# Loads of the next tokens' x2 issued singly and earlier in the projection, and one x tile split ahead of W's evictions

## The chip, the core and the metric

The kernel runs on one core of one Trainium2 chip. The metric is device time of one execution in microseconds (us), the median of several runs. All figures here come from those runs and from one profiled execution of the kernel. Engines are named as the profile names them: PE (TensorE matmuls), PEld (its weight loads), DVE (VectorE), ACT (ScalarE), POOL (GpSimd) and SP (SyncE, which here only issues DMAs).

## The reference

Three stages follow one another on 3072 tokens (4 batches of 768) with a model width of 512:

```
scores = q k^T / sqrt(64) + bias, kept only for the 8 global keys and the 96 local ones
x   = softmax(scores) v                       # 8 heads of 64, put side by side: 3072 x 512
x2  = (((x w1) * (x w2)) w3) w_out            # 512 -> 1024 -> 1024 -> 512
h   = x2 w_in                                 # 512 -> 2048
out = (h * cos(h)) w_out2                     # 2048 -> 512
```

Everything is float32.

## The kernel before, in words

**Precision.** Each float32 operand is split into a high and a low part in the format fp32r, and a product is three matmuls (high by high, high by low, low by high), issued by `mm3` (L419 in the rows). A split is a cast on ACT for the high part and a subtraction, nearly always on DVE, for the low part.

**First stage.** The weights w3 and w_out are multiplied into one matrix W (loop over `c` in `chunks`, 16 steps; `wmm` at L869 is its matmul, L877 and L878 are the ACT cast and the DVE subtraction that evict W). Attention for the first units (a unit is 128 tokens of two heads) runs in the same loop. `a_out` (L658 the ACT cast, L659 the DVE subtraction) splits a finished x tile of 384 tokens into the operand `xT`. In the loop's last step (`c` = 15) the program order on ACT and DVE is: the normalisation of one unit (`a_norm`; L599 and L602 on DVE, then L608 on ACT), W's four evictions, one decoding step of a weight (`decode`; L343 and L344 on ACT), and then `a_out` of the fourth x tile of the first token block. The next stage starts with `up`, whose twelve matmuls (four k by three) read the four x tiles in turn.

**Second stage.** Eight blocks of 384 tokens go through x w1, x w2 and W, while the remaining attention units and the decoding of w_in and w_out2 run beside them. x2 is written to DRAM (`x2s`).

**Third stage.** The tokens are taken in three passes `q` of 1024 tokens. Both products use a seven-product (Strassen) form on 2 x 2 blocks. In each pass:

- `phase_a` (eight steps k) computes h and the gate h * cos(h). Its right operands are B11, B22, B21 (blocks of x2) and T1 to T4 (their combinations), each in split form. They stand in single buffers.
- `phase_b`, the projection, walks the list `turn` of 56 pairs (n, k), called turns here. A turn is six matmuls. Turns 14 to 20 write to `k_ps`, turns 21 and 22 to `h_ps`, turn 23 to `k_ps`, and turn 24 begins a new product in `h_ps`. The left operand is a piece of w_out2 of 512 KB, which serves two turns; the right operand is `op`, made by `op_split` four turns ahead in program order (L1222 the ACT cast, L1223 the DVE subtraction), in a ring of six buffers. `fold` (L1240) forms the sums that later turns need.

In `phase_b` at turn `at`, the program order is: `pieces_to` (L1140 on SP: sends the piece of six pairs of turns ahead, once a buffer of its ring of eight is free), `op_split` of turn `at` + 4, the folds and gates due at this turn, the x2 work described next, and then the turn's matmuls, with an eviction where a product ends (`evict`).

**The x2 work.** The operands of the next pass are prepared inside `phase_b` of the passes 0 and 1. At turn 14 `x2_loads` sends B11, B22 and B21 (L933, 512 KB each) and then B12 into the buffer `r0` (L1365, 512 KB), all on SP. `x2_steps` is a list of 18 steps, each one instruction on DVE or ACT: first r1 = B22 - r0 (L959, it needs B22 and B12), then r0 = r0 - B11, and then the splits of B11, T1, T2, T3, B21, B22 and T4 (L946 on ACT, L948 on DVE). One step is taken at each of the turns 16, 21, 28 and every turn from 37 on but 44, 45 and 48. `r0` and `r1` take the two buffers that the last two gates of `phase_a` used; the gates' DVE multiplications that read them stand at turns 8 and 12.

All engines work through their instructions in the written order, so an instruction that waits holds up all that follow it on its engine. SP is in that respect an engine too.

Of the kernel before, what the change touches and what calls it, by code (L numbers as in the profile page):

```python
# [32 lines left out]
K1, M1, MO = DM // 128, DF1 // 128, DM // 128  # L33
# [238 lines left out]
def fused(ctx, tc, a_qk, a_v, a_v0, w3p, wo1p, w1p, w2p, winp, wo2p, out):  # L272
# [477 lines left out]
    with tc.manual_schedule():  # L750
# [8 lines left out]
        for o in "3A3A3A3A3A3A3A3ABBBBBBBB":  # L759
# [3 lines left out]
            else:  # L763
                n, m = ups.pop(0)
# [67 lines left out]
        def decode(n):  # L832
            for _ in range(n):
                next(steps_left, None)
# [27 lines left out]
        for c, (h, k) in enumerate(chunks):  # L862
            n = c - 1
            own = n if n < LEAD else -9
            if k == 0:
                W_ps = {m: p_mm.tile([128, 512], F32, tag="mm", name="mm") for m in range(4)}

            def wmm(m):
                nc.tensor.matmul(  # L869
                    W_ps[m], lhsT=wt["w3", c][:, m * 128:(m + 1) * 128], rhs=wt["wo1", k],  # L870
                    start=k == 0, stop=k == M1 - 1,
                )
                if k == M1 - 1:
                    t = wt["W", 4 * h + m] = wts.tile(
                        [128, 2, 512], F32R, tag="Wb" if h else "Wa", name="W", bufs=4
                    )
                    nc.scalar.copy(out=t[:, 0, :], in_=W_ps[m])  # L877
                    nc.vector.tensor_tensor(  # L878
                        out=t[:, 1, :], in0=W_ps[m], in1=t[:, 0, :].bitcast(F32), op=ALU.subtract
                    )  # L880

            a_load(own + 3)
            a_load_v(n - 1 if n > 2 else -1)
            if c % 3 == 0 and c < 12:
                bias_heads(*dists, range(2 * c // 3, 2 * c // 3 + 2))
            elif c == 10:
                tp.release()
            if n > 0:
                a_scores(own)
            if n > 0:  # L890
                a_load_plain(own + 2)
            a_values(n - 3)
            a_max(own)
            if c == 2 * M1 - 1:
                a_norm(n - 1, True)
                for m in range(4):
                    wmm(m)
            decode(1)
            a_out(n - 3)
            a_split_hi(own + 2)  # L900
            a_exp(own)
            a_split_lo(own + 2)
            if c < 2 * M1 - 1:
                wmm(0)
                wmm(1)
            a_transpose(n - 2)
            a_tcopy(n - 2)
            decode(1)
            if 1 <= n < 2 * M1 - 2:
                a_norm(n - 1, True, lambda: decode(1))  # L910
            else:
                decode(2)
            decode(2 if c < 8 else {14: 1, 15: 2}.get(c, 3))
            if c < 2 * M1 - 1:
                wmm(2)
                wmm(3)
# [8 lines left out]
            c = slice((2 * q + half) * TB2, (2 * q + half + 1) * TB2)  # L925
            return x2s[rows:rows + 2, :, c].rearrange("k p t -> p k t")

        def x2_loads(q):
            for name in ("B11", "B22", "B21"):
                t = x2c[name] = x2_pool[name].tile(  # L930
                    [128, 2, 2, TB2], F32R, tag=name, name=name, bufs=1
                )
                nc.sync.dma_start(out=t[:, :, 1, :].bitcast(F32), in_=x2_cols(name, q))  # L933
# [55 lines left out]
        for j in range(NB1):  # L989
            for i in range(UPB):  # L990
                sl = j * UPB + i
                n = sl + LEAD
# [71 lines left out]
        def one_bank():  # L1064
            return p_h.tile([128, TB2], F32, tag="h", name="h_ps")
# [207 lines left out]
        def phase_b(q):  # L1273

            final = q == NQ - 1
            base = (2 * q + 1) * (NP * 7 // 2)
            ps = {}
            extra = last_gates()
            for k in range(NP):
                for at, what in folds(k).items():  # L1280
                    extra[at] = extra.get(at, []) + what
            x2_next = None
            kept = {}

            def raw():
                return misc.tile([128, 2, TB2], F32, tag="raw", name="res", bufs=3)

            def total(out, p, q):
                nc.vector.tensor_tensor(out=out, in0=p, in1=q, op=ALU.add)

            def place(half, e):
                rows = slice(half * 256, half * 256 + 256)
                t = out[rows, (2 * q + e) * TB2:(2 * q + e + 1) * TB2]
                return t.rearrange("(i p) c -> p i c", p=128)

            def keep(name, t):

                kept[name] = t
                for i in range(2):
                    nc.scalar.copy(out=t[:, i, :], in_=ps["a"][i])  # L1300

            def evict(n):

                if n == 0:
                    keep("p0", raw())
                elif n == 1:
                    keep("p01", late.tile([128, 2, TB2], F32, tag="sum", name="sum", bufs=1))
                elif n == 4:
                    o = kept["p0"]
                    total(o, ps["c"], o)  # L1310
                    nc.sync.dma_start(out=place(0, 0), in_=o)
                elif n == 2:
                    keep("p012", raw())
                    o = raw()
                    for i in range(2):
                        total(o[:, i, :], ps["d"][i], kept["p012"][:, i, :])
                    nc.sync.dma_start(out=place(1, 1), in_=o)
                elif n == 5:
                    o = kept["p012"]
                    total(o, ps["b"], o)  # L1320
                    nc.sync.dma_start(out=place(0, 1), in_=o)
                elif n == 6 and not final:
                    o = kept["p01"]
                    for i in range(2):
                        total(o[:, i, :], ps["d"][i], o[:, i, :])
                    nc.sync.dma_start(out=place(1, 0), in_=o)

            def evict_last(i):

                o = kept["p01"]  # L1330
                for h, queue_ in enumerate((nc.scalar, nc.sync)):
                    c = slice(h * 256, h * 256 + 256)
                    total(o[:, i, c], ps["d"][i][:, c], o[:, i, c])
                    queue_.dma_start(out=place(1, 0)[:, i, c], in_=o[:, i, c])

            def step(n, k, which):
                bank = home_of[n]
                w = pieces[q, n, k // 2][:, k % 2]
                x = ops[n, k]
                for i in which:  # L1340
                    if k == 0 and n in opens and i == 0:
                        if bank in "ad":
                            ps[bank] = [one_bank(), one_bank()]
                        else:
                            t = two_banks()
                            ps[bank] = t
                    mm3(
                        ps[bank][i] if bank in "ad" else ps[bank][:, i, :],
                        [(w[:, i, 0, :], w[:, i, 1, :], x[:, 0, :], x[:, 1, :])],
                        n in opens and k == 0, k == NP - 1, n not in opens,  # L1350
                    )

            for at, (n, k) in enumerate(turn):
                pieces_to(base + pairs_of.index((n, k // 2)) + 6)
                if at + 4 < len(turn):
                    op_split(*turn[at + 4])
                for what in extra.get(at, ()):
                    what()
                if at == 14 and not final:
                    x2_loads(q + 1)  # L1360
                    r0, r1 = (
                        late.tile([128, 2, TB2], F32, tag="x2f", name="x2f", bufs=2)
                        for _ in range(2)
                    )
                    nc.sync.dma_start(out=r0, in_=x2_cols("B12", q + 1))  # L1365
                    x2_next = x2_steps(r0, r1)
                if x2_next and (at in (16, 21, 28) or at > 36 and at not in (44, 45, 48)):
                    some(x2_next, 1)
                if q == 0 and at in (34, 38, 42):
                    flags_of[0] = next(steps_f)  # L1370
                if final and at >= len(turn) - 4:
                    if at == len(turn) - 1:
                        for i in range(2):
                            for kk in range(NP - 4, NP):
                                step(n, kk, (i,))
                            evict_last(i)
                else:
                    step(n, k, range(2))
                    if k == NP - 1:
                        evict(n)  # L1380
            return x2_next
# [95 lines left out]
```

## Time and profile before

| What | us |
|---|---|
| median of 3 runs (lowest to highest) | 1095.5 (1094.88 to 1096.44) |
| the profiled execution, its own time | 1096.8 |
| its span, first to last instruction | 1094.9 |
| PE busy | 1073.8 (98%) |
| DVE busy | 832.1 (76%) |
| ACT busy | 731.4 (67%) |
| POOL busy | 237.5 (22%) |
| mean granted TensorE clock | 0.993 |

The span is cut by stages: the first ends at about 93 us, the second at about 615 us, and the third fills the rest. Within the third, `phase_b` of pass 0 runs from about 691 to 776 us and that of pass 1 from about 852 to 936 us. A granted clock of 1.00 is 2.4 GHz, one of 0.50 is 1.2 GHz.

### The profile page before, as it was taken

The page shows a single profiled execution, that of the slowest core. Times are in us where ns is not written, and L with a number is a line of the kernel's source. Part 1 is how long each engine was busy: PE and PEld are TensorE (multiplying, and loading weights), DVE is VectorE, ACT ScalarE, POOL GpSimd, SP SyncE. Part 2 cuts the span into 40 slices and gives each one's busy share as a digit, 9 for nine tenths or more (in the row PEclk, how much of TensorE's full clock was granted, in tenths as well). Part 3 has the DMA queues.
Part 4 walks back from the last instruction along what each step waited for, and adds up shares of the span by engine and source line. Part 5 has one row for each costly group of instructions (what it writes and reads, how often), then busy time and mean ns, then how long its engine had stood idle before and what let it go on. Part 6 is the DMA issues. An engine that isn't in the chain of part 4 may idle for free.

```text
span 1094.9 us, 17774 instructions
## 1 busy us (share of the span) xinstructions
PE 1073.8 (98%) x5922; PEld 933.1 (85%) x5922; DVE 832.1 (76%) x1812; ACT 731.4 (67%) x1487; POOL 237.5 (22%) x249
## 2 busy tenths in 40 slices
PE   8999999999999999999999999989999989999997
PEld 5557899999999999999999988868888868888886
DVE  8887767878788787787826388868788869688984
ACT  7998867777677676676734388736378736478652
POOL 0000011111211111121100078300078200178100
PEclk9999999999999999999999999989999989999999
DMA  9865466666666756666452456564855565855563
GB/s 332 287 192 171 142 200 200 204 227 197 221 202 204 239 189 221 200 213 212 138 193 95 144 192 192 188 219 168 292 194 194 175 240 190 276 192 193 173 195 115
DMA packets 88308, 219.24 MB, mean 200 GB/s; under 512 B 9488, under 2 KB 26384, under 8 KB 88208
## 3 DMA queue, kind: packets, MB, share of 16 engines
q1 hardware_dynamic: 87696, 217.44, 59.5%
q8 instruction: 49, 0.80, 0.3%
q10 hardware_dynamic: 512, 0.58, 0.2%
q14 instruction: 51, 0.42, 0.1%
HBM read 176.04 MB, written 41.94 MB: 199 GB/s over the span
## 4 chain that ended last, share of the span: by engine, by line
PE 55%; DMA 2%; DVE 1%; ACT 1%; issue 0%; POOL 0%; DVEq 0%; ACTq 0%; POOLq 0%
PE h_ps L419 36%; PE mm L419 11%; PE k_ps L419 5%; DMA x2f<-x2s 1%; PE x_ps L644 1%; PE pt_ps L617 0%; DMA o2s<-ap 0%; PE pt_ps L619 0%; PE s_ps L559 0%; PE s_ps L555 0%; DVE x2f L959 0%; ACT e L589 0%; DVE op L1223 0%; ACT raw L344 0%; DVE xT L659 0%
## 5 line engine op out<-in xcount | busy, mean ns | idle before, releaser
L419 PE MATMUL h_ps<-op,piece 128*128 128x512 f32 x720 | 171.4, 397 | 9.8 <-DVE op L1223 9.8
L610 POOL TENSOR_SCALAR e<-e,st 128x232 f32<-128x232 f32 x148 | 76.1, 525 | 476.9 <-DVE st L602 385.0
L419 PEld LDWEIGHTS h_ps<-op,piece 128*128 128x128 f32 x720 | 137.8, 192 | 39.7 <-DVE op L1223 10.6
L419 PE MATMUL mm<-xT,wA 128*128 128x384 f32 x768 | 146.8, 340 | 0.5 <-ACT xT L658 0.4
L419 PE MATMUL mm<-xT,wB 128*128 128x384 f32 x768 | 146.2, 339 | 0.0
L419 PE MATMUL mm<-ab,W 128*128 128x384 f32 x768 | 146.2, 340 | 0.0
L419 PE MATMUL h_ps<-T,piece 128*128 128x512 f32 x576 | 138.4, 389 | 0.0
L419 PEld LDWEIGHTS mm<-xT,wA 128*128 128x128 f32 x768 | 130.9, 188 | 3.2 <-issue 1.8
L419 PEld LDWEIGHTS mm<-ab,W 128*128 128x128 f32 x768 | 131.1, 188 | 2.4 <-issue 2.4
L419 PEld LDWEIGHTS mm<-xT,wB 128*128 128x128 f32 x768 | 130.9, 188 | 2.1 <-issue 2.1
L419 PEld LDWEIGHTS h_ps<-T,piece 128*128 128x128 f32 x576 | 108.1, 188 | 22.5
L1113 POOL TENSOR_TENSOR gr<-r,gr 128x1024 f32<-128x1024 f32 x21 | 50.5, 2405 | 290.5 <-ACT r L1108 289.0
L419 PE MATMUL h_ps<-B,piece 128*128 128x512 f32 x432 | 105.7, 389 | 0.0
L419 PEld LDWEIGHTS h_ps<-B,piece 128*128 128x128 f32 x432 | 81.1, 188 | 16.8
L589 ACT ACTIVATE e<-e,top 128x232 f32<-128x232 f32 (+1 forms) x192 | 89.3, 467 | 2.2 <-DVE top L578 2.1
L522 ACT CAST hh<-qk 128x720 fp32r<-128x720 f32 x74 | 58.9, 796 | 46.7 <-PE s_ps L559 42.5
L578 DVE CUSTOM_DVE_ANT_0 e<-s_ps,bias 128x232 f32<-128x232 f32 (+1 forms) x192 | 64.9, 374 | 14.3 <-PE s_ps L559 8.6
L419 PE MATMUL k_ps<-op,piece 128*128 128x512 f32 x288 | 67.9, 392 | 0.0
L419 PEld LDWEIGHTS k_ps<-op,piece 128*128 128x128 f32 x288 | 54.9, 191 | 11.6
L869 PE MATMUL mm<-wo,w 128*128 128x512 f32 x128 | 61.2, 606 | 1.1 <-DVE wo L360 1.1
L1105 ACT ACTIVATE r<-r 128x1024 f32<-128x1024 f32 x48 | 51.0, 1062 | 16.6 <-DVE r L1099 16.6
L1222 ACT CAST op<-gr 128x512 fp32r<-128x512 f32 x72 | 42.9, 621 | 28.3 <-PE h_ps L419 11.2
(136 smaller groups left out, 1968.6 us busy)
## 6 DMA issues: line engine op xcount, KB each, us to landing
piece<-a_s SPq DMA_DIRECT2D x84, 512.0 KB, 4.2
piece<-o2s SPq DMA_DIRECT2D x84, 512.0 KB, 3.9
qk<-in_a_qk SPq DMA_DIRECT2D x74, 360.0 KB, 3.4
a_s<-ap SPq DMA_DIRECT2D x56, 256.0 KB, 2.5
o2s<-ap SPq DMA_DIRECT2D x56, 256.0 KB, 2.5
v<-in_a_v SPq DMA_DIRECT2D x95, 128.0 KB, 3.4
raw<-in_w3p SPq DMA_DIRECT2D x16, 512.0 KB, 5.0
raw<-in_winp SPq DMA_DIRECT2D x16, 512.0 KB, 3.5
```

Source lines behind the costliest of these rows:

```text
L419: nc.tensor.matmul(ps, lhsT=l, rhs=r, start=first and i + e == 0, stop=last and i == n - 1 and e == 2, skip_group_check=more,)
L522: nc.scalar.copy(out=hh[n], in_=qk_raw[n])
L578: nc.vector.tensor_tensor_reduce(out=es[n][:, e, :w], in0=sp[:, e, :w], in1=bias[:, 2 * p + e, :], scale=-0.125, scalar=3.0e38, op0=ALU.ad ...
L589: nc.scalar.activation(es[n][:, e, :w], es[n][:, e, :w], ACTF.Exp, bias=top[:, n, e:e + 1], scale=-1.0, accum_out=sts[n][:, 0, e:e + 1],)
L610: nc.gpsimd.tensor_scalar(x, x, st[:, 1, e:e + 1], 1.0, ALU.mult, ALU.mult)
L644: nc.tensor.matmul(x[e * 64:(e + 1) * 64, i * 128:(i + 1) * 128], lhsT=vt[:kk, c, e * 64:(e + 1) * 64], rhs=pt[:kk, e, c, :], start=c == 0 ...
L869: nc.tensor.matmul(W_ps[m], lhsT=wt["w3", c][:, m * 128:(m + 1) * 128], rhs=wt["wo1", k], start=k == 0, stop=k == M1 - 1,)
L1105: nc.scalar.activation(self.r, self.r, ACTF.Abs)
L1113: engine.tensor_tensor(out=self.h, in0=self.r, in1=self.h, op=ALU.mult)
L1222: nc.scalar.copy(out=t[:, 0, :], in_=x)
```

## The change

Three edits:

- In the last step of the first stage's loop, `a_out` moves from behind W's evictions and the decoding step to ahead of the normalisation and the evictions.
- In `phase_b`, the loads of B11, B22 and B21 go out singly at turns 1, 4 and 7, where all three went out at turn 14. The load of B12 goes out at turn 13, where it was fourth at turn 14.
- The list of x2 steps is no longer served at turn 16. Its first step falls on turn 21, its second on 28, and each later step one served turn later than before; the eighteenth falls on turn 55, the last one.

```diff
             if c == 2 * M1 - 1:
+                a_out(n - 3)
                 a_norm(n - 1, True)
                 for m in range(4):
                     wmm(m)
             decode(1)
-            a_out(n - 3)
+            if c < 2 * M1 - 1:
+                a_out(n - 3)
...
-        def x2_loads(q):
-            for name in ("B11", "B22", "B21"):
+        def x2_loads(q, names=("B11", "B22", "B21")):
+            for name in names:
...
-                if at == 14 and not final:
-                    x2_loads(q + 1)
+                if at in (1, 4, 7) and not final:
+                    x2_loads(q + 1, (("B11", "B22", "B21")[at // 3],))
+                if at == 13 and not final:
                     r0, r1 = (
                         late.tile([128, 2, TB2], F32, tag="x2f", name="x2f", bufs=2)
                         for _ in range(2)
                     )
                     nc.sync.dma_start(out=r0, in_=x2_cols("B12", q + 1))
                     x2_next = x2_steps(r0, r1)
-                if x2_next and (at in (16, 21, 28) or at > 36 and at not in (44, 45, 48)):
+                if x2_next and (at in (21, 28) or at > 36 and at not in (44, 45, 48)):
                     some(x2_next, 1)
```

## Rows read from the trace of the kernel before

**Rows 1.** The list of waits: who waited, for whom, total us, times, longest.

```profile
PE h_ps L419 <- DVE op L1223: 9.8, 2, 5.2
...
DVE x2f L959 <- DMA x2f<-x2s: 15.1, 2, 7.9
```

**Rows 2.** The chain that ended last, start and length in us, around 715 us.

```profile
715.37 8.37 DMA x2f<-x2s
723.76 1.23 DVE x2f L959
724.98 0.61 DVE op L1223
```

**Rows 3.** Timeline of pass 0's projection: start, length, engine, line, count, [idle before].

```profile
710.52 9.68 PE L419 MATMUL k_ps<-op,piece 128*128 128x512 f32 x42
711.04 1.22 DVE L1113 TENSOR_TENSOR jj<-r,jj 128x1024 f32<-128x1024 f32 x1
...
713.80 1.45 SPq L933 DMA_DIRECT2D B<-x2s  x3
...
720.04 0.39 PE L419 MATMUL h_ps<-op,piece 128*128 128x512 f32 x1
...
725.64 5.06 PE L419 MATMUL h_ps<-op,piece 128*128 128x512 f32 x11 [5.21 <-DVE op L1223]
...
732.19 10.16 PE L419 MATMUL h_ps<-op,piece 128*128 128x512 f32 x44
```

**Rows 4.** The same view of pass 1's projection.

```profile
880.99 0.39 PE L419 MATMUL h_ps<-op,piece 128*128 128x512 f32 x1
...
885.96 5.06 PE L419 MATMUL h_ps<-op,piece 128*128 128x512 f32 x11 [4.58 <-DVE op L1223]
...
892.55 7.65 PE L419 MATMUL h_ps<-op,piece 128*128 128x512 f32 x33
```

**Rows 5.** Windows of 1 us: busy time of each engine, PEclk, DMA share, GB/s.

```profile
722.00:723.00 1.00, 0.00 (x0) 0.00 (x0) 0.00 (x0) 0.00 (x0) 0.00 (x0) 1.00 1.05 426
...
726.00:727.00 1.00, 1.00 (x3) 0.80 (x3) 1.00 (x3) 0.10 (x1) 0.00 (x0) 0.50 0.00 0
...
732.00:733.00 1.00, 1.00 (x6) 0.83 (x5) 1.00 (x3) 0.29 (x1) 0.00 (x0) 1.00 0.87 348
```

**Rows 6.** Timeline of SP alone, pass 0's projection: issues of pieces.

```profile
688.89 3.04 SPq L1140 DMA_DIRECT2D piece<-o2s  x2
694.33 0.32 SPq L1140 DMA_DIRECT2D piece<-o2s  x1
...
699.77 4.43 SPq L1140 DMA_DIRECT2D piece<-o2s  x2
...
709.35 0.32 SPq L1140 DMA_DIRECT2D piece<-o2s  x1
713.43 0.32 SPq L1140 DMA_DIRECT2D piece<-o2s  x1
```

**Rows 7.** Times from issue to landing of the pieces, 680 to 730 us.

```profile
DMA to landing us min/median/max: 3.2/4.2/8.8
```

**Rows 8.** Timeline of pass 0's projection around turn 48.

```profile
764.22 1.87 DVE L1223 TENSOR_TENSOR op<-jj,op 128x512 fp32r<-128x512 f32 x3
...
765.30 9.94 PE L419 MATMUL h_ps<-op,piece 128*128 128x512 f32 x43
```

**Rows 9.** Timeline of the end of the first stage.

```profile
90.50 0.87 ACT L608 ACTIVATE e<-e,st 128x232 f32<-128x232 f32 x2 [0.83 <-DVE st L602]
...
92.62 1.83 PE L419 MATMUL mm<-xT,wA 128*128 128x384 f32 x9
...
94.82 0.56 DVE L659 TENSOR_TENSOR xT<-x_ps,xT 128x384 fp32r<-128x384 f32 x1
...
95.43 0.62 PE L419 MATMUL mm<-xT,wA 128*128 128x384 f32 x2
...
96.25 2.36 PE L419 MATMUL mm<-xT,wA 128*128 128x384 f32 x12
```

## What I expected, and why

> **What bounds the kernel now.** The table of busy times comes first: PE is busy for 1073.8 of 1094.9 us, DVE and ACT for much less. So PE sets the time, and a change is worth what it does to PE's idle time and to PE's pace. The list of waits comes second: of PE's 21 us of idle time, 9.8 lie in two waits of the third stage, both for the low part of an operand from DVE, and DVE itself waited twice, 15.1 us in all, for the DMA of the buffer `x2f` [rows 1]. The chain that ended last comes third, to see that these two belong together: it leads from the DMA through DVE's first x2 step and one operand split back to PE [rows 2]. DVE stood at turn 16's x2 step, and the operand of turn 21 was queued behind it. The timeline of the two places gives the size, and one-microsecond windows show that the wait costs more than its length: the granted clock is still 1.00 while PE stands, then it is 0.50 (1.2 GHz) when PE starts again, and it is back at 1.00 only some seven microseconds later [rows 5].
>
> **Term 1: the two stalls.** I count matmuls from the code and times from the timeline. Turns 14 to 20 are 42 matmuls, from 710.52 to the start of turn 21 at 720.04, so one takes 9.52 / 42 = 0.2267 us at the full clock [rows 3]. Turns 21 to 23 are 18 matmuls, which at that pace take 4.08 us. They took 732.19 - 720.04 = 12.15 us in pass 0 [rows 3], which is 8.07 too many, and 892.55 - 880.99 = 11.56 us in pass 1 [rows 4], 7.48 too many. Together 15.55 us. Of this 5.21 + 4.58 = 9.79 us is standing [rows 3, 4], and the other 5.76 us is the low clock after it. If the stall goes, both go.
>
> Does it go? The x2 step at turn 16 is removed, so nothing on DVE waits between turns 14 and 20. Its place in the work moves to turn 21, and so do its DMAs. I follow them on SP, which sends a piece as soon as PE frees a buffer. The piece sent at turn 0 goes out at 688.89, the one of turn 4 at 694.33, that of turn 7 at 699.77, that of turn 13 at 709.35 and that of turn 14 at 713.43 [rows 6]. Today all four x2 loads stand behind the last of these [rows 3]. After the change each stands right behind the piece of its turn: B11 at about 689.2, B22 at 694.7, B21 at 700.1 and B12 at 709.8. Do the single buffers delay them? B11, B21 and B22 are read last in the final step of `phase_a`, as the first, fifth and sixth of its seven products. That step ends where the projection begins (14 turns of 1.36 us before 710.52, so 691.5), and a product of six matmuls takes 1.36 us. The last reads therefore end at about 683.3, 688.7 and 690.1, before the loads. The buffer of B12 is free after a gate's multiplication at turn 8 of DVE's order. If it is the other of the two buffers, it is free after turn 12's, which DVE ended at 712.3 [rows 3]. So B12 goes out between 709.8 and 712.3.
>
> A piece, of the same 512 KB, takes 4.2 us to land in the middle and 8.8 at the worst, in a stretch that has the four x2 loads in it [rows 7]; B12 itself took 8.4 as the last of the four [rows 2]. B12 then lands between 714.0 and 721.1, most likely at 714. DVE wants it at turn 21. It falls idle today at 723.76 - 7.9 = 715.9 [rows 1, 2], in front of turn 16's step; from there to turn 21's step it has five splits (of the operands of turns 21 to 25) and four folds to do, of 0.61 us each [rows 2], so the step comes at about 721.4 or, if ACT's casts wait for free buffers, later. Even the late end of the load is in time. And if it were not, the first matmul behind the step is that of turn 26, at 720.04 + 5 x 1.36 = 726.9: less the step (1.23, [rows 2]) and the split (0.61, [rows 2]) DVE could wait until 725.1 before PE notices. I take no wait.
>
> **Term 2: the loads in a busier stretch.** SP sends three loads ahead of pieces. A piece sent at 694.33 serves turn 14 at 710.52 [rows 3, 6]; it lands in 4.2 us, so 12.0 us are to spare. The DMAs have moved 426 GB/s in a window [rows 5]; at that rate 512 KB take 1.23 us, and one load ahead of a piece costs it between this and 4.2 us. I take nothing: the spare time hides it. The Trainium skill (DMA: Bandwidth & Descriptors, section on queues, rings and completion order) speaks against moving loads ahead of pieces: each DMA engine takes the descriptors of one issuer's ring in order, so a piece stands behind the whole load, and no run here has shown that order yet. By that rule the piece is later by a load's data time, and the sum is the same, as long as the spare time holds.
>
> **Term 3: the steps moved by one.** In the turns 37 to 55 the same steps are taken, each one served turn later. Turn 48 is where DVE is closest to PE: its operand is ready at about 764.8 (the first of three splits that begin at 764.22, some 0.62 each), and PE wants it at 765.30 [rows 8], so 0.46 us is to spare. Up to turn 48 DVE does four of these two-block steps both before and after the change, but the last of the four, T2's subtraction of 1.2 us, moves from turn 42 to 43. I count the same amount of DVE work ahead of turn 48's split in either order, so it should be ready at about the same time. Bounds: a gain of nothing (PE does not wait there) and a loss of 1.22 - 0.46 = 0.76 us in each of two passes, 1.5 us. I take nothing.
>
> At turn 55 the last step now stands before the last eviction. T4 is wanted six products into the next pass, 6 x 1.36 = 8.2 us later; it hides there.
>
> **Term 4: the x tile.** PE does the twelve matmuls of the first `up` from 92.62 to 95.43 + 0.62 = 96.05, so in 3.43 us; the next twelve, undisturbed, take 2.36 [rows 9]. 1.07 us is lost, to the missing fourth tile. After the change ACT does this tile's cast in the 0.83 us in which it waits for DVE today, before the normalisation at 90.50 [rows 9]. But on DVE the tile's subtraction (0.56 us, [rows 9]) now stands ahead of the normalisation's two small steps, ACT's normalisation waits for these, W's casts stand behind that, and the first `up` waits for the first bank that W's eviction frees. So the start moves back by about 0.56 us and the twelve run through: 1.07 - 0.56 = 0.5 us won, of which the next transposes lose some 0.15, as ACT's copy that frees their bank also comes later. Bounds: 1.07 won, if the bank is free by other slack, and 0.56 lost, if the fourth tile was not what the matmuls waited for. I take 0.35 won, nearest to the row of the 0.56.
>
> **Sum.** 15.55 + 0 + 0 + 0.35 = 15.9 us. The profiled execution took 1096.8 us, its span and 1.9 around it, so 1080.9. It lies 1.3 above the median of the runs, so against the median: 1095.5 - 15.9 = 1079.6 us, a gain of 1.45%.
>
> **Rivals.**
>
> *The wait comes back in part (0.05).* B12 lands after 725, because the loads' landing is slower beside pieces than any row shows, or SP is held at turn 13 by a buffer. It would move the wait from turn 16's step to turn 21's. For it: pieces beside the loads did take up to 8.8 us. Against it: it would take over 12 us. With half of the stalls left, 1095.5 - 7.8 - 0.35 = 1087.4 us.
>
> *DVE is late at turn 48 (0.06).* Term 3's loss in full: 1079.6 + 1.5 = 1081.1 us. For it is the small spare time, against it the equal amount of DVE work.
>
> *Pieces starve PE: slower (0.03).* The place is turns 14 to 24, the price is paid where pieces stand behind x2 loads. It decides from the point at which the three loads hold a piece up by more than the 12.0 us to spare. At 6.5 us each (halfway between 4.2 and 8.8, [rows 7]) and one after the other, they hold it up by 19.5, PE stands 7.5 us, and with the low clock after it, in term 1's proportion 15.55 / 9.79, that is 11.9 us in each pass: 1079.6 + 23.8 = 1103.4 us. Against it: the loads overlap, all four landed within the 10 us from 713.80 to 723.74 [rows 2, 3].
>
> *The change doesn't do what it says (0.02).* The step still waits as long, for a reason that the trace puts on the DMA and which is another, and the stall is only moved: 1095.5 - 0.35, so about 1095 us.
>
> **How the numbers follow.** My forecast of 1079.6 us holds 0.84. Its own spread comes from term 4 (0.7 better, 0.9 worse) and about 0.8 us of the runs. The range of 1078.2 to 1083.0 takes in the forecast, term 4's bounds and DVE's lateness at turn 48, and leaves out the other three rivals. A measurement of this kernel can tell about 0.2% (2.2 us) from no change. Faster by more than that are the forecast, the wait in part and DVE at turn 48: 0.95. Within it lies the change that does nothing, 0.02, and slower is the starved PE, 0.03.
>
> **What would show it.** Right: no wait of DVE for `x2f` and none of PE for an operand of the third stage; a granted clock of 1.00 in every window of both projections; the 18 matmuls of turns 21 to 23 in about 4.1 us; B loads that go out between pieces about 5 us apart; a first `up` of about 2.4 us that starts half a microsecond later after W. Wrong: a DVE wait at L959 that is longer than 3 us, a PE wait for a piece, a dip of the clock elsewhere, or a gain near 10 us with the clock still low.

## The result and the profile after

| | before | changed |
|---|---|---|
| median (lowest to highest), us | 1095.19 (1094.32 to 1096.44) | 1081.04 (1080.11 to 1081.29) |
| profiled execution, its own time | 1096.8 | 1080.91 |
| its span | 1094.9 | 1079.0 |
| PE busy | 1073.8 | 1067.1 |
| mean granted clock | 0.993 | 0.999 |

The changed kernel takes 0.9868 of the time of the kernel before, with a 95% interval of 0.9851 to 0.9885. That is 14.15 us by the medians and 15.9 us between the two profiled executions. The forecast was 1079.6 us, in a range of 1078.2 to 1083.0.

In the changed kernel's list of waits, PE has no entry left for an operand of the third stage (the 9.8 us of [rows 1]), and DVE has none for `x2f`; the longest of PE are the start of the kernel and small ones of the first stage:

```profile
PE warm L847 <- POOL ident masks.py:199: 2.5, 1, 2.5
PE mm L869 <- DVE wo L360: 1.7, 2, 1.1
...
PE mm L419 <- DVE W L878: 0.4, 1, 0.4
```

Its timeline in pass 0's projection answers [rows 2, 3, 6]. Lines behind the edits are two or three higher now: L961 is the first x2 step, L935 the loads of B11, B22 and B21, L1368 that of B12.

```profile
689.35 1.29 SPq L935 DMA_DIRECT2D B<-x2s  x1
...
694.79 0.43 SPq L935 DMA_DIRECT2D B<-x2s  x1
...
700.23 0.43 SPq L935 DMA_DIRECT2D B<-x2s  x1
...
709.86 0.37 SPq L1368 DMA_DIRECT2D x2f<-x2s  x1
...
720.12 2.88 PE L419 MATMUL h_ps<-op,piece 128*128 128x512 f32 x12
...
721.29 1.22 DVE L961 TENSOR_TENSOR x2f<-B,x2f 128x1024 f32<-128x1024 f32 x1
...
724.20 11.04 PE L419 MATMUL h_ps<-op,piece 128*128 128x512 f32 x48
```

The four loads go out singly. DVE's first x2 step has no idle time in front of it. The 18 matmuls of turns 21 to 23 take 724.20 - 720.12 = 4.08 us, where they took 12.15. Pass 1 goes the same way, in 877.00 - 872.91 = 4.09 us where it took 11.56:

```profile
872.91 2.88 PE L419 MATMUL h_ps<-op,piece 128*128 128x512 f32 x12
...
877.00 11.04 PE L419 MATMUL h_ps<-op,piece 128*128 128x512 f32 x48
```

The granted clock is 1.00 in every window of both projections. Where [rows 5] had PE standing or at half the clock, it is now busy throughout at the full one:

```profile
720.00:724.00 4.00, 4.00 (x20) 3.30 (x19) 3.69 (x6) 2.73 (x5) 0.00 (x0) 1.00 0.65 224
724.00:728.00 4.00, 4.00 (x19) 3.34 (x18) 3.94 (x8) 1.87 (x3) 0.00 (x0) 1.00 0.78 289
```

The end of the first stage, against [rows 9]:

```profile
90.17 0.56 DVE L659 TENSOR_TENSOR xT<-x_ps,xT 128x384 fp32r<-128x384 f32 x1
...
91.10 0.87 ACT L608 ACTIVATE e<-e,st 128x232 f32<-128x232 f32 x2 [0.96 <-DVE st L602]
...
93.21 2.35 PE L419 MATMUL mm<-xT,wA 128*128 128x384 f32 x12 [0.44 <-DVE W L878]
...
95.96 2.34 PE L419 MATMUL mm<-xT,wA 128*128 128x384 f32 x12
```

The twelve matmuls run through in 2.35 us, but they start at 93.21 where they started at 92.62, because the tile's subtraction pushed the normalisation back (91.10, it was 90.50). The next twelve start at 95.96 where they started at 96.25: 0.29 us won at this place.

### The profile page after: what moved, and what is told of

Read it like the earlier page. It is cut to its first block, busy times and chain, and to the rows that moved or that the text cites. A ratio compares the mean times of both kernels' runs of the same rounds, so it can differ in the third digit from the quotient of the medians.

```text
span 1079.0 us, 17774 instructions
## 1 busy us (share of the span) xinstructions
PE 1067.1 (99%) x5922; PEld 928.9 (86%) x5922; DVE 832.2 (77%) x1812; ACT 731.2 (68%) x1487; POOL 238.0 (22%) x249
## 4 chain that ended last, share of the span: by engine, by line
PE 70%; DVE 0%; POOL 0%; ACT 0%; issue 0%; DVEq 0%; POOLq 0%
PE h_ps L419 36%; PE mm L419 22%; PE k_ps L419 6%; PE x_ps L644 2%; PE pt_ps L617 1%; PE s_ps L559 1%; PE s_ps L555 1%; PE pt_ps L619 1%; DVE sum L1291 0%; DVE xT L659 0%; DVE kl L529 0%; POOL e L610 0%; DVE hh L532 0%; ACT xT L658 0%; DVE st L599 0%
## 5 line engine op out<-in xcount | busy, mean ns | idle before, releaser
L419 PE MATMUL h_ps<-op,piece 128*128 128x512 f32 x720 | 166.2, 389 | 0.0
L419 PEld LDWEIGHTS h_ps<-op,piece 128*128 128x128 f32 x720 | 135.0, 188 | 28.1
```

The source lines that it names most:

```text
L419: nc.tensor.matmul(ps, lhsT=l, rhs=r, start=first and i + e == 0, stop=last and i == n - 1 and e == 2, skip_group_check=more,)
```

## The experiments

The theory: the gain is the two stalls with the low clock behind them, and nothing waits in their place; the x tile gives a few tenths. The rivals in question were which edit does it, whether the clock's share goes with the length of the stall, and whether pieces suffer. Kernels that were run together share the runs of the kernel before: median 1096.01 us for the first four, 1096.35 us for the last four.

### The loads without the x tile

```diff
             if c == 2 * M1 - 1:
-                a_out(n - 3)
                 a_norm(n - 1, True)
...
-            if c < 2 * M1 - 1:
-                a_out(n - 3)
+            a_out(n - 3)
```

> The change without its first edit: a_out stays behind W's evictions; the early loads and the later first use stay. My theory puts all but 0.35 us of the gain here: about 0.4 us above the changed kernel's 1081.0, so 1081.4 us, no DVE wait for x2f, clock 1.00 in both projections. Rival (the x tile carries a share): the time is more than 1 us above the changed kernel's.

Measured: 1080.79 us (1080.15 to 1081.49), 0.9858 of the kernel before (0.9842 to 0.9874). No difference from the whole change that can be told; no DVE wait for `x2f`, and a mean clock of 1.00. The gain is in the loads and the steps. The rival, more than 1 us above the changed kernel, did not come. The few tenths of the x tile don't show in a time.

### The x tile without the loads

The edit of the diff's first part alone, on the kernel before.

> The first edit alone: a_out ahead of the normalisation and W's evictions, the x2 loads as before. Theory: 0.35 us faster than the kernel before, so about 1094.8 us; the two stalls of 5.2 and 4.6 us with their low clock stay. Rival: the later start of the first up costs as much as the tile wins, so no difference, and the first twelve matmuls and the next transposes end no earlier than before.

Measured: 1096.17 us, 0.9996 of the kernel before (0.9987 to 1.0006): no difference, and 0.35 us lies inside that interval, so the time can't tell theory from rival. The trace has the same order of events at W's end as the changed kernel, and its second twelve matmuls start at 96.07, where they started at 96.25 in the kernel before. The run was worth more for another thing. Both stalls are there, but in pass 1 the clock came back sooner. Its timeline in the two passes:

```profile
720.44 0.39 PE L419 MATMUL h_ps<-op,piece 128*128 128x512 f32 x1
726.38 5.06 PE L419 MATMUL h_ps<-op,piece 128*128 128x512 f32 x11 [5.55 <-DVE op L1225]
...
732.93 3.36 PE L419 MATMUL h_ps<-op,piece 128*128 128x512 f32 x14
```

```profile
881.73 0.39 PE L419 MATMUL h_ps<-op,piece 128*128 128x512 f32 x1
886.07 4.11 PE L419 MATMUL h_ps<-op,piece 128*128 128x512 f32 x11 [3.95 <-DVE op L1225]
...
891.38 4.92 PE L419 MATMUL h_ps<-op,piece 128*128 128x512 f32 x21
```

Turns 21 to 23 lost 12.49 - 4.08 = 8.41 us in pass 0, of which 5.55 standing and 2.86 after it; in pass 1 they lost 9.65 - 4.08 = 5.57, of which 3.95 standing and 1.62 after it. The windows of pass 1 show the clock back at 1.00 by 889, three microseconds after PE's start at 886.07; in the kernel before PE started at 725.64 and the clock was back by 732 [rows 3, 5]:

```profile
886.00:887.00 1.00, 0.93 (x2) 0.83 (x3) 1.00 (x3) 0.00 (x0) 0.00 (x0) 0.50 0.12 45
...
888.00:889.00 1.00, 1.00 (x4) 0.81 (x3) 1.00 (x3) 0.39 (x1) 0.00 (x0) 0.55 0.00 0
889.00:890.00 1.00, 1.00 (x5) 0.79 (x5) 1.00 (x3) 1.00 (x3) 0.00 (x0) 1.00 0.47 86
```

### Early loads, first step at turn 16 as before

```diff
-                if x2_next and (at in (21, 28) or at > 36 and at not in (44, 45, 48)):
+                if x2_next and (at in (16, 21, 28) or at > 36 and at not in (44, 45, 48)):
```

> The changed kernel with the first x2 step back at turn 16; the loads stay early. Theory: B12 goes out at 709.9 and lands before 715.9, where DVE comes to the step, so nothing waits and the time is that of the changed kernel, 1081.0 us within 0.5. Rival (the later first use is what removes the stall): DVE waits at turn 16 and PE stands for some part of 5 us in each of two passes, 1084 to 1095 us.

Measured: 1080.64 us (1080.46 to 1081.06), 0.9856 of the kernel before (0.9839 to 0.9872). Its timeline:

```profile
715.41 1.22 DVE L961 TENSOR_TENSOR x2f<-B,x2f 128x1024 f32<-128x1024 f32 x1
...
719.66 2.88 PE L419 MATMUL h_ps<-op,piece 128*128 128x512 f32 x12
```

B12 goes out at 709.39 and lands 4.5 us later, at 713.9. The step runs at 715.41, with no idle time before it, and PE goes through turn 21. The early loads without the later step take the whole gain, as far as a time can tell.

### Late loads, first step at turn 21

```diff
-                if at in (1, 4, 7) and not final:
-                    x2_loads(q + 1, (("B11", "B22", "B21")[at // 3],))
-                if at == 13 and not final:
+                if at == 14 and not final:
+                    x2_loads(q + 1)
```

> The changed kernel with all four loads back at turn 14; the first x2 step stays at turn 21. Theory: B12 lands at about 723.7, DVE comes to the step at 721.3 and waits 2.4 us, the split of turn 26 is ready at 725.6 where PE wants it at 726.9, so PE does not stand: 1081.0 us within 0.5, with a DVE wait and no PE wait. Rival (the early loads are what removes the stall): PE stands behind that wait, at least 1 us in each pass, and the clock falls: 1084 to 1095 us.

Measured: 1081.64 us (1080.84 to 1081.81), 0.9862 of the kernel before (0.9845 to 0.9878). The list of waits and the timeline:

```profile
DVE x2f L961 <- DMA x2f<-x2s: 4.7, 2, 2.7
```

```profile
715.74 0.44 SPq L1367 DMA_DIRECT2D x2f<-x2s  x1
...
720.41 2.88 PE L419 MATMUL h_ps<-op,piece 128*128 128x512 f32 x12
...
724.41 1.22 DVE L961 TENSOR_TENSOR x2f<-B,x2f 128x1024 f32<-128x1024 f32 x1 [2.74 <-DMA x2f<-x2s]
724.49 7.87 PE L419 MATMUL h_ps<-op,piece 128*128 128x512 f32 x34
```

DVE still waits for B12, 4.7 us in the two passes, and PE does not notice: it runs from turn 21 through turn 26, the first behind the step, without a stop. The later first use without the early loads takes the whole gain too, as far as a time can tell. So each of the two edits is enough, and the other adds spare time only. That spare time is small with either one alone. With the early loads, B12 was there 1.5 us before DVE came to the step. With the later step, the split of turn 26 was ready at about 726.2 and PE wanted it at about 727.2 (724.49 and two turns of 1.36): 1.0 us.

### A short stall

The first step at 16 as above, and the loads at turn 14 in another order:

```diff
-                if at in (1, 4, 7) and not final:
-                    x2_loads(q + 1, (("B11", "B22", "B21")[at // 3],))
-                if at == 13 and not final:
+                if at == 14 and not final:
+                    x2_loads(q + 1, ("B22",))
...
                     nc.sync.dma_start(out=r0, in_=x2_cols("B12", q + 1))
+                    x2_loads(q + 1, ("B11", "B21"))
...
-                if x2_next and (at in (21, 28) or at > 36 and at not in (44, 45, 48)):
+                if x2_next and (at in (16, 21, 28) or at > 36 and at not in (44, 45, 48)):
```

> The changed kernel with the first x2 step back at turn 16 and all four loads at turn 14, but B22 and B12, which that step needs, ahead of B11 and B21. Theory: the two land at about 719.6 after an issue at 713.8, DVE waits 3.7 us, and PE stands about 1.0 us in each pass. If the low clock comes only with long standing, the time is 2 us above the changed kernel's 1081.0, so 1083.0, and the granted clock stays at 1.00; if the clock falls with any stall and costs 0.59 us for each us of standing as in the kernel before, 1084.2 us.

Measured: 1085.19 us (1085.0 to 1085.94), 0.9901 of the kernel before (0.9885 to 0.9918).

```profile
720.05 0.39 PE L419 MATMUL h_ps<-op,piece 128*128 128x512 f32 x1
720.26 1.23 DVE L961 TENSOR_TENSOR x2f<-B,x2f 128x1024 f32<-128x1024 f32 x1 [4.38 <-DMA x2f<-x2s]
...
722.14 2.79 PE L419 MATMUL h_ps<-op,piece 128*128 128x512 f32 x11 [1.70 <-DVE op L1225]
...
726.13 9.23 PE L419 MATMUL h_ps<-op,piece 128*128 128x512 f32 x40
```

```profile
722.00:723.00 1.00, 0.86 (x4) 0.73 (x5) 1.00 (x3) 0.09 (x1) 0.00 (x0) 1.00 1.05 426
723.00:724.00 1.00, 1.00 (x6) 0.83 (x5) 1.00 (x3) 0.90 (x2) 0.00 (x0) 1.00 1.05 428
```

PE stands for 1.70 us (1.57 in pass 1), and the clock is 1.00 in every window of both projections. Turns 21 to 23 take 726.13 - 720.05 = 6.08 us, 2.00 too many (1.86 in pass 1), so a stall of this length costs itself and 0.3 us beside, and nothing for the clock. The time is 4.15 us above the changed kernel's for these 3.86. Both theories had counted on a shorter stall, because B12 landed at about 720.2 and not at 719.6. With the stalls as they came, 3.27 us in all, a clock that stays gives 1084.3 us and one that falls with any stall 1086.2. The 1085.19 measured lies between them, so the windows decide, not the time.

### A long stall

The first step at 16, and all four loads at turn 16, behind one more piece:

```diff
-                if at in (1, 4, 7) and not final:
-                    x2_loads(q + 1, (("B11", "B22", "B21")[at // 3],))
-                if at == 13 and not final:
+                if at == 16 and not final:
+                    x2_loads(q + 1)
...
-                if x2_next and (at in (21, 28) or at > 36 and at not in (44, 45, 48)):
+                if x2_next and (at in (16, 21, 28) or at > 36 and at not in (44, 45, 48)):
```

> The changed kernel with the first x2 step back at turn 16 and all four loads at turn 16, one piece later than in the kernel before. The loads go out about 2.7 us later, and so PE stands about 2.7 us longer, 7.9 and 7.3 us. If the low clock costs a fixed amount after long standing (2.9 us in each pass), the time is 2 x 2.7 us above the kernel before less 0.35, about 1100 us; if it grows with the standing (1.59 us lost for each us), 2 x 4.3 above, about 1103.5 us.

Measured: 1100.97 us (1099.47 to 1101.59), 1.0043 of the kernel before (1.0029 to 1.0057): slower by 4.6 us at the medians. Its timeline in the two passes:

```profile
719.48 0.39 PE L419 MATMUL h_ps<-op,piece 128*128 128x512 f32 x1
728.32 5.06 PE L419 MATMUL h_ps<-op,piece 128*128 128x512 f32 x11 [8.45 <-DVE op L1225]
...
735.17 5.17 PE L419 MATMUL h_ps<-op,piece 128*128 128x512 f32 x22
```

```profile
883.93 0.39 PE L419 MATMUL h_ps<-op,piece 128*128 128x512 f32 x1
891.88 4.19 PE L419 MATMUL h_ps<-op,piece 128*128 128x512 f32 x11 [7.57 <-DVE op L1225]
...
897.30 4.92 PE L419 MATMUL h_ps<-op,piece 128*128 128x512 f32 x21
```

In pass 0, turns 21 to 23 take 735.17 - 719.48 = 15.69 us; 15.69 - 4.08 = 11.61 us are lost, 8.45 standing and 3.16 after it. In pass 1 it is 9.29, 7.57 and 1.72. The stall grew by three microseconds, and what follows it did not grow with it. A fixed price is the nearer of the two theories, but it is not one price. The table sets the six long stalls of three kernels beside the two short ones; each row is one profiled execution.

| kernel, pass | standing | lost after it |
|---|---|---|
| short stall, 0 and 1 | 1.70, 1.57 | 0.30, 0.29 |
| before, 0 and 1 | 5.21, 4.58 | 2.86, 2.90 |
| x tile alone, 0 and 1 | 5.55, 3.95 | 2.86, 1.62 |
| long stall, 0 and 1 | 8.45, 7.57 | 3.16, 1.72 |

What is lost after a long stall goes with how long the clock stays low once PE runs again. In the long stall of pass 0 PE starts at 728.32 and the clock comes back in the first of these windows; in pass 1 it starts at 891.88 and the clock comes back in the second:

```profile
734.00:735.00 1.00, 1.00 (x5) 0.79 (x4) 1.00 (x3) 0.04 (x1) 0.00 (x0) 0.75 0.56 139
894.00:895.00 1.00, 1.00 (x4) 0.76 (x4) 1.00 (x3) 0.58 (x2) 0.00 (x0) 0.54 0.00 0
```

That is about 6.2 us at half the pace in pass 0 and 3.0 in pass 1, and half of that, 3.1 and 1.5 us, is nearly all of the 3.16 and 1.72. The other four long stalls agree: 5.5 to 5.6 us where 2.86 to 2.90 was lost, 2.8 where 1.62 was. What decides when the clock comes back was not tested.

### Three loads in front of the pieces

```diff
-                if at in (1, 4, 7) and not final:
-                    x2_loads(q + 1, (("B11", "B22", "B21")[at // 3],))
+                if at == 1 and not final:
+                    x2_loads(q + 1)
```

> The changed kernel with B11, B22 and B21 sent together at turn 1; B12 at 13, first step at 21. Theory: pieces have 12 us to spare, so three loads of 512 KB ahead of a piece delay its landing by up to 4 us and PE never waits for one: 1081.0 us within 0.5. It bears on the rule that one ring is taken in order: the piece sent behind the three loads should then land later than the usual 4 us. Rival (pieces starve PE): a PE wait for a piece DMA in turns 14 to 24, 1084 us or more.

Measured: 1080.47 us (1079.57 to 1081.24), 0.9854 of the kernel before (0.9837 to 0.987). The three loads go out from 689.45, and the piece sent at 691.8, right behind them, took this long to land:

```profile
DMA to landing us min/median/max: 8.5/8.5/8.5
```

In the changed kernel the same piece, behind one load, took this long:

```profile
DMA to landing us min/median/max: 4.4/4.4/4.4
```

So loads do hold up the pieces behind them, by 4.1 us here. The three loads, sent at 689.45, 690.6 and 691.1, took this long, in the order in which they were sent:

```profile
DMA to landing us min/median/max: 6.7/7.1/8.0
```

So the loads and the piece landed in the order of their issue, at about 696.2, 697.7, 699.1 and 700.3. That agrees with what the Trainium skill (DMA: Bandwidth & Descriptors, section on queues, rings and completion order) says of a ring taken in order. It does not show that order is all: the first load took 6.7 us, where B11 of the changed kernel, sent at the same place, took 5.0, so what was sent behind it may have slowed it too. This run doesn't tell order from sharing. PE's list of waits has no piece in it: 4.1 is well inside the 12.0 us that the prediction found to spare for the piece of turn 14. Sending the loads singly is not what gains the time.

### The x tile's subtraction behind the normalisation's

```diff
-                a_out(n - 3)
-                a_norm(n - 1, True)
+                between = iter((None, lambda: a_out(n - 3)))
+                a_norm(n - 1, True, lambda: (next(between) or (lambda: None))())
```

> The changed kernel with a_out moved on DVE behind the normalisation's two small steps (L599, L602) and still ahead of W's evictions; ACT's order is unchanged. Theory: the tile's subtraction then fills DVE's idle time before W's first eviction, so the normalisation, W's casts and the first up start 0.56 us earlier, PE waits no 0.4 us for W, and the next transposes come about 0.5 us earlier: 0.5 us below the changed kernel, about 1080.5 us. Rival: the start after W is set by something else, and the time is the changed kernel's.

Measured: 1080.46 us (1079.54 to 1081.05), 0.9853 of the kernel before (0.9837 to 0.987).

```profile
90.54 0.54 DVE L659 TENSOR_TENSOR xT<-x_ps,xT 128x384 fp32r<-128x384 f32 x1
90.72 0.87 ACT L608 ACTIVATE e<-e,st 128x232 f32<-128x232 f32 x2 [0.46 <-DVE st L602]
...
92.83 2.35 PE L419 MATMUL mm<-xT,wA 128*128 128x384 f32 x12
...
95.58 1.64 PE L419 MATMUL mm<-xT,wA 128*128 128x384 f32 x8
```

The mechanism is the expected one. ACT's normalisation starts at 90.72 and the first twelve matmuls at 92.83, where the changed kernel has 91.10 and 93.21, and the next twelve begin 0.38 us earlier. The time is 0.6 us below the changed kernel's, and 0.01 below that of the kernel with three loads at turn 1, which ran beside it with the tile as the change has it. Whether it is the faster version can't be told from these runs.

## Why the prediction was right, point by point

**The bound and the stalls (term 1)** came out as worked out. PE's 9.8 us of waits and the low clock after them are gone, and it was right to count both: of the 15.55 us the standing is 9.8. The times read from SP's queue were good: B11, B22, B21 and B12 were forecast at 689.2, 694.7, 700.1 and 709.8 and went out at 689.35, 694.79, 700.23 and 709.86; the first x2 step was forecast at 721.4 and ran at 721.29. The spare time that I gave for the late B12 was put to the test by the late loads with the step at 21: DVE waited 2.74 us and PE nothing. (720.04 + 5 x 1.36 is 726.84, not 726.9; nothing hangs on it.)

One reading of the clock was loose. It did not stay at 1.00 while PE stood, and after PE's start at 725.64 it was not low for some seven microseconds. Two more windows of the kernel before show that it had fallen by the end of the standing, and that it was back at about 731.1, 5.5 us after the start:

```profile
724.00:725.00 1.00, 0.00 (x0) 0.00 (x0) 1.00 (x2) 0.00 (x0) 0.00 (x0) 0.66 0.55 221
...
731.00:732.00 1.00, 1.00 (x6) 0.82 (x5) 1.00 (x2) 0.36 (x1) 0.00 (x0) 0.93 0.29 41
```

Running 5.5 us at half the pace loses 2.75 of the 2.86 us that pass 0 lost behind the standing. So the 5.76 us of the prediction are the low clock up to a tenth or so in each pass. The size of the term does not change by that, since it was counted from matmuls.

**What the prediction did not separate** is which of the two edits does it. It costed them together. Each alone is enough, the early loads because B12 is there when DVE comes by at turn 16, the later step because DVE has then made the operands that PE needs next.

**The loads in a busier stretch (term 2)** cost nothing, even three at a time. The rival of the starved pieces had a real effect as its base, 4.1 us of delay for a piece, and stayed far from the point from which it decides.

**The steps moved by one (term 3)** cost nothing. The changed kernel's timeline at turn 48, against [rows 8]:

```profile
755.78 2.49 DVE L1225 TENSOR_TENSOR op<-jj,op 128x512 fp32r<-128x512 f32 x4
...
757.32 2.88 PE L419 MATMUL h_ps<-op,piece 128*128 128x512 f32 x12
```

The first of these four splits, turn 48's, ends at about 756.4 (2.49 / 4 after 755.78), 0.9 us ahead of PE, where 0.46 was to spare before.

**The x tile (term 4)** was forecast at 0.35 us with the start moved back by 0.56. The start moved by 0.59 and 0.29 us was won at that place in the trace. It did not last: turn 21 of pass 0 starts at 720.12, against 720.04 before [rows 3], so in these two executions the tenths were gone by then, and no time shows them.

**The rivals.** The wait did not come back, DVE was not late, no piece starved PE, and the change does what it says. The price that I gave the starved pieces, though, took the clock's share as proportional to the standing (15.55 / 9.79). The short and the long stall show that this is wrong.

**The sum and the last step.** The gain between the two profiled executions is 1096.8 - 1080.91 = 15.9 us, the sum of the prediction. That it fits to the tenth is partly luck. At turn 24 of pass 1 the changed kernel is 892.55 - 877.00 = 15.55 us ahead, which is term 1 alone; the rest of the 15.9 arose behind that turn and not in the x tile. The miss of 1.4 us is in the last step, in which I took 1.3 us off because the profiled execution of the kernel before lay that much above the median of its runs. The changed kernel's profiled execution lies at its median. In the two later comparisons the kernel before had medians of 1096.01 and 1096.35 us, so its profiled execution lay only 0.8 and 0.4 above those, and the 1.3 us came in good part from a median of three runs that was low. The time lost behind a stall differs by over 1 us between stalls (2.86 and 1.62 in the table above), which is enough for such differences between executions. One pair of traces agrees with that: the profiled execution of the x tile alone took 1095.03 us, 1.77 less than that of the kernel before, and lost 1.57 less in its two stalls (8.41 + 5.57 against 15.55). That this is where the differences between runs of the kernel before come from was not shown, since no other execution of it has a trace here.

## What to carry to other kernels

Read a stall of PE as the count of matmuls in the stretch against their full pace, not by the length of the wait: 9.8 us of waiting were 15.6 us of loss here. Where an engine works in order, ask what stands behind the waiting instruction; moving the load earlier and moving the step later are two cures for one wait, and one may be enough. Before taking a difference of a microsecond between a profiled execution and a median of three into a forecast, see how far the kernel's runs spread: the 25 of the kernel before lie between 1094.32 and 1097.75 us.

## What the runs showed that I had not expected

The time lost behind a stall does not go in proportion to its length. Stalls of 1.6 and 1.7 us left the clock at 1.00 and lost 0.3 us beside themselves. Stalls of 3.95 to 8.45 us were all followed by a stretch at 0.50 (1.2 GHz), which cost 1.6 to 3.2 us, and the longest two had one of the dearest and one of the cheapest, by how soon the clock came back after PE's start. The Trainium skill (TensorE: Matmul & The Clock Gate, section on HAM oscillation) describes the long case, a stream of matmuls that comes out of a wait at half the clock; the rows agree with it, and they add that the waits of 1.6 and 1.7 us in this stream stayed free of it.
